# Hiding three of eight head groups of keys and queries in the padding rows of the other five

## The chip, the cores and the metric

The kernel runs on one core of one Trainium2 chip. The metric is device time in microseconds of one execution, the median of several runs. The profile shown is of one execution that was also timed.

## The reference

The model interleaves an attention block (A) and a token-mixing MLP (B), twice, over the same weights. There are S = 2048 tokens of D = 640, H = 32 heads of Dh = 20, and F = 1536. All arrays are bf16.

```python
def _A_ref(x, wqkv, wo):
    qkv = (x @ wqkv).reshape(B, S, 3, H, Dh)          # then split in q, k, v
    scores = jnp.einsum("bhqd,bhkd->bhqk", q, k) * (Dh ** -0.5)
    o = jnp.einsum("bhqk,bhkd->bhqd", softmax(scores), v)
    return o.transpose(0, 2, 1, 3).reshape(B, S, D) @ wo

def _B_ref(x, w1, b1, w2, b2):
    u = gelu(jnp.einsum("bsd,sf->bdf", layernorm(x), w1) + b1)
    return (jnp.einsum("bdf,fs->bds", u, w2) + b2).transpose(0, 2, 1)

x = x + _A_ref(layernorm(x), A_wqkv, A_wo)
x = x + _B_ref(layernorm(x), B_w1, B_b1, B_w2, B_b2)
# and both lines once more
```

Each layer has 32 heads times 2048 x 2048 scores, so 134 million exponentials.

## The kernel before, in words

**Heads in groups.** Four heads make a group, so there are NG = 8 groups. A head has 20 dimensions and takes a strip of 32 partitions: head j of a group lies on partitions 32j to 32j+19, and partitions 32j+20 to 32j+31 hold zeros. The padded weights are `wk_pad` and `wq_pad` (5 tiles of 128 input features, 8 groups, 128 columns); the padding columns are cleared by DVE (L1570) and ACT (L1579), and the others are copied in from `w_raw` (L1589 on ACT for groups 0 to 3, L1591 on DVE for groups 4 to 7). A projection (`proj_fill`, matmuls at L1199) multiplies one group's weights with 512 tokens of the normalised, transposed input `hT` (a view of `hh`), in five matmuls, and a copy (L377 for keys, L379 for queries, which also scales) brings the result from PSUM to `KT[:, g, tokens]` or `QTq[:, g, :]`. There are 8 groups times 4 blocks of tokens, for keys and for queries, in each layer.

**Scores and exponentials.** A cell is one head, 512 queries and 128 keys. `s_matmul` (L718) computes it as one matmul that contracts a strip of 32 partitions, at a position of the array of its own for each head of the group. Cells go into PSUM tiles `S` of three and two cells in turn, and ACT takes the exponential of a whole tile (L788, output `P`). Some cells go to DVE and POOL instead, by integer arithmetic on the bits of the number: they are computed into `Dt`, DVE takes them out (`ew`, L570), and a row of passes makes `ey` and then `Pd` (L600, L605, L623, L625), of which POOL can do parts (L676 for `ey`, L659 for `Pd`). [...] P times V (L1349) accumulates in `acc`, for four heads side by side.

**Order of the work.** The order on every engine is written by a planner in Python that runs while the program is built. It keeps its own clock for PE, DVE and ACT and puts "fills" (projections, output projection, first MLP matmuls) into the holes that PE has between scores, by due times. Where PE has been less busy than a floor (`FLOOR`, over `SPAN_US` = 3.413 us of its clock), it adds waves of four matmuls with zero weights (`zero_wave`, L777). A score matmul counts there as a quarter of the array. The DMAs on SP's queue are ordered by the framework; each waits on one of eight semaphores in turn, so for the DMA eight places ahead of it.

**Early runs.** Each attention starts before all tokens are there: groups 0 to 3 (`EG = 4`) and query blocks 0 and 1 are computed as tokens come in. Their partial sums lie in the parts of `KT` that belong to groups 4 to 7 (`part_view`), which are projected when the early runs of a block have ended. In layer 0 (`TokenFeed`) the tokens come from the input, in 16 tiles of 128 (`x0in`): each is normalised on DVE (L901 to L922) with a power on POOL (`rstd`, L918), transposed on PE, and projected. In layer 1 (`MixFeed`) they come from the MLP of layer 0. The weights `wk_pad` and `wq_pad` are built once, in layer 0.

**First MLP matmuls.** Rows of w1 times the normalised tokens (L1090, "mm1", accumulated by DVE at L1098) run as fills in three parts, by the tokens that are already there; `mid_rows` says how many of the 12 rows are begun before the last tokens are known.

## Time and profile before

| | |
|---|---|
| median of 3 runs | 1747.16 us (1746.76 to 1747.34) |
| the profiled execution's own time | 1747.74 us |
| span of its profile, first to last instruction | 1745.7 us |
| ACT exponentials (L788) | 1428 tiles, 1615.9 us busy |
| attention of layer 0, first to last exponential | 16.23 to 815.50 us |
| attention of layer 1, exponentials | 852.03 to 1675.9 us |
| projections of K and Q (L1199) | 243 + 237 matmuls into misc, 43 + 49 into Dt recorded |
| zero waves into acc (L777) | 4112 matmuls, 320.1 us busy |
| DVE copies of K and Q (L377, L379) | 64 + 64, about 0.68 us each |
| POOL passes for Pd (L659) | 337 of 0.62 us |

Times are microseconds from the first instruction of the span. "Busy" of a group is the time in which at least one of its instructions ran; the mean duration of one is longer where they overlap. A matmul's duration includes its way through the array, and the next one starts before it ends. PE's waits for weights ("PEld ... issue") are no loss by themselves.

### The profile page before, as it was taken

Reading aid. Unit: us, or ns where it says so; the run is one execution under the profiler, and the core shown is the slowest. Engines: PE = TensorE matmul, PEld = TensorE weight load, DVE = VectorE, ACT = ScalarE, POOL = GpSimd, SP = SyncE. Lnnn points to the kernel's source line nnn. Section 1 sums busy time; section 2 is a strip of 40 time slices with the busy share of each in tenths; the row PEclk is TensorE's granted clock in tenths of the full one; section 3 lists DMA queues with packets and bytes.
Section 4 is the critical chain, followed back from the end, with each engine's and each line's share of the span. In section 5 each row is a group of like instructions: output and inputs, shape, how many; then the busy total and the mean of one; then the engine's idle time right before and its main releaser. Section 6 shows DMA issues by size and latency. Waiting matters only on the chain.

```text
span 1745.7 us, 42946 instructions
## 1 busy us (share of the span) xinstructions
PE 1660.8 (95%) x17674; PEld 664.5 (38%) x17756; DVE 1541.2 (88%) x2511; ACT 1665.7 (95%) x1497; POOL 593.5 (34%) x952
## 2 busy tenths in 40 slices
PE   8999999999999999999999999999999999999999
PEld 3333333333333344444534433333333333444455
DVE  8789999999999999998544479999999999999973
ACT  9999999999999999999789999999999999999970
POOL 3133443443444333342000023434435443433310
PEclk9999999999999999999999999999999999999999
DMA  5000000000122010133412200001001220211245
GB/s 131 15 14 1 1 2 2 24 24 2 35 67 82 26 36 14 40 86 109 145 49 75 70 6 2 1 2 39 24 2 61 69 75 17 92 30 29 79 126 174
DMA packets 103060, 81.84 MB, mean 47 GB/s; under 512 B 51024, under 2 KB 87504, under 8 KB 102864
## 3 DMA queue, kind: packets, MB, share of 16 engines
q1 hardware_dynamic: 97328, 71.22, 13.8%
q0 software_dynamic: 5536, 7.88, 1.5%
q8 instruction: 138, 2.26, 0.6%
q14 instruction: 58, 0.48, 0.1%
HBM read 55.48 MB, written 23.59 MB: 45 GB/s over the span
## 4 chain that ended last, share of the span: by engine, by line
ACT 52%; PE 23%; issue 23%; DVE 1%; DMA 0%; SPq 0%; another core or an unknown queue 0%; POOL 0%; ACTq 0%; DVEq 0%
ACT P L788 52%; PE S L718 7%; PE acc L1349 3%; PE ya L1804 2%; PE misc L1199 2%; PE acc L777 2%; PE misc L1090 2%; PE Dt L1199 1%; PE um L1791 1%; PE ya L1813 1%; PE yb L1804 1%; PE misc L1177 1%; PE misc L1223 0%; PE Dt L1723 0%; DMA x0in<-in_A_x_dram 0%
## 5 line engine op out<-in xcount | busy, mean ns | idle before, releaser
L788 ACT ACTIVATE P<-S 128x1536 bf16<-128x1536 f32 (+1 forms) x1428 | 1615.9, 1370 | 10.6 <-PE S L718 10.3
L718 PE MATMUL S<-QTq,KT 32*128 32x512 bf16 (+1 forms) x4456 | 577.2, 336 | 66.9 <-ACT P L788 49.6
L676 POOL TENSOR_SCALAR ey<-ew 128x512 f16<-128x512 uint16 x511 | 317.3, 621 | 622.4 <-DVE ey L605 257.7
L718 PEld LDWEIGHTS <-KT 32*128 32x128 bf16 x5140 | 233.6, 91 | 523.4 <-issue 494.3
L570 DVE TENSOR_SCALAR ew<-Dt 128x512 int32<-128x512 f32 x528 | 359.4, 681 | 22.9 <-PE Dt L718 14.8
L1349 PE MATMUL acc<-P,Vaug 128*32 128x512 bf16 (+1 forms) x4436 | 362.1, 343 | 0.3 <-issue 0.3
L605 DVE SCALAR_TENSOR_TENSOR ey<-ey,ew 128x1024 int16<-128x1024 f16 x264 | 331.6, 1256 | 1.6
L777 PE MATMUL acc<-zr,zw 128*32 128x512 bf16 x4112 | 320.1, 383 | 1.2 <-POOL zr L155 1.2
L659 POOL TENSOR_SCALAR Pd<-ew 128x512 int16<-128x512 int16 x337 | 208.1, 620 | 233.6 <-DVE ey L605 74.9
L718 PE MATMUL Dt<-QTq,KT 32*128 32x512 bf16 (+1 forms) x684 | 202.9, 333 | 0.0
L600 DVE TENSOR_TENSOR ey<-ey 128x1024 f16<-128x1024 f16 x264 | 190.1, 720 | 1.5 <-POOL ey L676 0.3
L1349 PEld LDWEIGHTS <-Vaug 128*32 128x32 bf16 x5120 | 102.1, 94 | 171.8 <-issue 160.1
L777 PEld LDWEIGHTS <-zw 128*32 128x32 bf16 x4328 | 109.5, 96 | 92.8 <-issue 48.7
L623 DVE TENSOR_TENSOR Pd<-Pd,ey 128x1024 int16<-128x1024 int16 (+1 forms) x196 | 126.5, 645 | 6.4 <-POOL Pd L659 4.8
L625 DVE SCALAR_TENSOR_TENSOR Pd<-ew,ey 128x1024 int16<-128x1024 int16 (+1 forms) x123 | 122.4, 995 | 0.0
L918 POOL TENSOR_TENSOR rstd<-veps,mhalf 128x1 f32<-128x1 f32 x60 | 44.9, 749 | 210.9 <-DVE veps L916 188.6
L1349 PE MATMUL acc<-Pd,Vaug 128*32 128x512 bf16 (+1 forms) x684 | 103.7, 336 | 0.2 <-DVE Pd L623 0.2
L1199 PE MATMUL misc<-hh,wq_pad 128*128 128x512 bf16 x243 | 73.9, 383 | 2.8 <-issue 1.4
L1090 PEld LDWEIGHTS <-w1st 128*128 128x128 bf16 x672 | 52.4, 97 | 58.1 <-issue 45.4
L1199 PE MATMUL misc<-hh,wk_pad 128*128 128x512 bf16 x237 | 71.8, 383 | 2.2 <-issue 1.6
L1139 PE MATMUL misc<-wo_pad,attnT 128*128 128x320 bf16 x384 | 72.8, 302 | 0.0
L1090 PE MATMUL misc<-x1last,w1st 128*128 128x320 bf16 x384 | 71.4, 302 | 0.0
(144 smaller groups left out, 1187.4 us busy)
## 6 DMA issues: line engine op xcount, KB each, us to landing
w2s<-in_B_w_dram SPq DMA_DIRECT2D x16, 768.0 KB
uacc<-ustg POOLq DMA_DIRECT2D x24, 320.0 KB, 2.6
x1in<-xd SPq DMA_DIRECT2D x24, 320.0 KB
w1st<-in_B_w_dram SPq DMA_DIRECT2D x24, 256.0 KB
xd<-x2s SPq DMA_DIRECT2D x16, 320.0 KB
xin<-xd SPq DMA_DIRECT2D x16, 320.0 KB
w1st<-in_B_w_dram SPq DMA_DIRECT2D x21, 192.0 KB
xd<-x1s SPq DMA_DIRECT2D x12, 320.0 KB
```

What stands on the lines that cost most here:

```text
L570: nc.vector.tensor_scalar(out=w[:, slot, :], in0=Dt[:, :], scalar1=127.0 * FIX, scalar2=0.0, op0=ALU.add, op1=ALU.max)
L600: nc.vector.tensor_tensor(out=y, in0=y, in1=y, op=ALU.mult)
L605: nc.vector.scalar_tensor_tensor(out=box["t"][:, 0:512 * k], in0=y[:, 0:512 * k], scalar=MANT_C * MANT_K ** 2, in1=frac, op0=ALU.add, op1= ...
L623: nc.vector.tensor_tensor(out=bits, in0=bits, in1=t, op=ALU.add)
L659: after_vector(nc.gpsimd.tensor_scalar(out=bits, in0=whole, scalar1=128.0, scalar2=0.0, op0=ALU.mult, op1=ALU.add))
L676: return engine.tensor_scalar(out=out_ap, in0=in_ap, scalar1=MANT_K / FIX, scalar2=-MANT_K * MANT_S, op0=ALU.mult, op1=ALU.add)
L718: pe(nc.tensor.matmul(out_ap[:, c0:c0 + w], lhsT=KT[32 * j:32 * j + 32, g, kt * 128:(kt + 1) * 128], rhs=get_QT(st, qb)[32 * j:32 * j + 32 ...
L777: pe(nc.tensor.matmul(bank[32 * j:32 * j + 32, 0:w], lhsT=zw[:], rhs=zr[:, :, 0:64].to_broadcast([128, w // 64, 64]), start=start, stop=st ...
L788: nc.scalar.activation(out=P[:, 0:ncs, :].rearrange("p a b -> p (a b)"), in_=St[:, 0:ncs, :].rearrange("p a b -> p (a b)"), func=ACT.Exp, ...
L1090: pe(nc.tensor.matmul(t[:, 0:w], lhsT=w1_of[(p, ft)][:, sti, :], rhs=rows_in[sti][:, c0:c1], start=(sti == 0), stop=(sti == n_in - 1)))
L1199: pe(nc.tensor.matmul(t[:, :], lhsT=wpad[:, dt_, g, :], rhs=hT[:, dt_, tb * 512:(tb + 1) * 512], start=(dt_ == 0), stop=(dt_ == NDT - 1)))
L1349: pe(nc.tensor.matmul(acc[32 * j:32 * j + 32, a0:a0 + w], lhsT=Vaug[:, (kt * H + hh_) * VW:(kt * H + hh_) * VW + 32], rhs=P[:, slot, c0:c0 ...
```

## The change

Only groups 0 to 4 (`NP = 5`) are projected. The 12 padding rows of each of their strips now hold dimensions of the heads of groups 5, 6 and 7 (`HIDDEN`): 12 dimensions of group 5 in the gaps of group 0, 8 in those of group 1, and so on. The same five matmuls produce both. DMAs on SP's queue (`carry`, one for each strip) then move these rows to the places of groups 5 to 7 in `KT` and `QTq`, over partitions: 28 DMAs for the keys of a layer, 28 for each of the four query blocks.

Scores now contract the 20 rows of a head (`32 * j + DH`), because the rows behind them hold other heads' data.

In layer 0 the first projections of group 0 (the first 512 tokens) run before the gaps of its weights are filled; for these tokens two extra projections (`apart_fill`) are made later into tiles `apart`. The gaps are filled by 14 small copies on POOL, so the second half of the raw weights is now loaded before the input tiles 4 and 5. The padding is no longer cleared, but for group 0.

The partial sums of the early runs move (`homes`): block 0 into the parts of groups 4 and 6, block 1 into 5 and 7; the late groups are computed in the order 6, 4, 5, 7. A move is issued when its sources have been copied from PSUM and its place is free, and the planner books `MOVE_US`, 0.4 us for each DMA and 3.0 us to land. `mid_rows` of layer 0 goes from 0 to 2.

```diff
+NP = 5
+GAP = 32 - DH
+HIDDEN = {5: ((0, 0, 12, 0), (1, 0, 8, 12)), 6: ((2, 0, 12, 0), (3, 0, 8, 12)),
+          7: ((4, 0, 12, 0), (1, 8, 4, 12), (3, 8, 4, 16))}
+MOVE_US = (0.4, 3.0)
...
-    wq_pad = wperm.tile([128, NDT, NG, 128], BF16, name="wq_pad")
-    wk_pad = wperm.tile([128, NDT, NG, 128], BF16, name="wk_pad")
+    wq_pad = wperm.tile([128, NDT, NP, 128], BF16, name="wq_pad")
+    wk_pad = wperm.tile([128, NDT, NP, 128], BF16, name="wk_pad")
+    apart = [wperm.tile([128, 512], BF16, name=f"apart{i}") for i in range(2)]
...
+        homes = {EQ[0]: (4, 6), EQ[1]: (5, 7)}
+        rest = [6, 4, 5, 7]
...
-                pe(nc.tensor.matmul(out_ap[:, c0:c0 + w], lhsT=KT[32 * j:32 * j + 32, g, kt * 128:(kt + 1) * 128],
-                                    rhs=get_QT(st, qb)[32 * j:32 * j + 32, g, q0:q0 + w], start=True, stop=True,
+                pe(nc.tensor.matmul(out_ap[:, c0:c0 + w], lhsT=KT[32 * j:32 * j + DH, g, kt * 128:(kt + 1) * 128],
+                                    rhs=get_QT(st, qb)[32 * j:32 * j + DH, g, q0:q0 + w], start=True, stop=True,
...
+        def carry(dst, src, c0, c1, first, n, dim):
+            for j in range(4):
+                nc.sync.dma_start(out=dst[32 * j + dim:32 * j + dim + n, c0:c1],
+                                  in_=src[32 * j + DH + first:32 * j + DH + first + n, c0:c1])
...
+        def move_keys(L):
+            need = [("K", p[0], tb) for p in HIDDEN[L] for tb in range(NQB)]
+            if feed.regap and L == 5:
+                need.append(("G", 0))
+            owner = next(qb for qb in EQ if L in homes[qb])
+
+            def free():
+                return (feed.gate_late() and all(k in drained for k in need) and
+                        not any(qg[0] == owner for qg in early_left))
...
         def proj_fill(kind, g, tb, prio, ready, gate=None, fed=False):
+            if g >= NP:
+                return
...
     class TokenFeed:
         groups = 4
+        regap = True
...
-        mid_rows = 0
+        mid_rows = 2
...
             load_w(self.wv[:, 0], 2 * D)
+            load_raw(0, 1)
+            load_raw(1, 1)
             for tt in range(4, 6):
                 load_x(tt)
...
+            def gap_copies(i, tile_):
+                for L, parts in HIDDEN.items():
+                    for t_, first, n, dim in parts:
+                        if t_ == tile_:
+                            src = raw[(i, 1)][:].rearrange("p a (h i) -> p a h i", i=DH)[:, :, 4 * (L - 4):4 * (L - 4) + 4, dim:dim + n]
+                            nc.gpsimd.tensor_copy(out=gap_of(i, tile_, first, n), in_=src)
...
+            gaps_at(10.8, [(0, 1)])
+            gaps_at(12.0, [(1, 1), (0, 2), (1, 2), (0, 3), (1, 3)])
+            gaps_at(19.0, [(0, 4), (1, 4)])
+            gaps_at(19.0, [(0, 0), (1, 0)], lambda: ("K", 0, 0) in cx.kready and ("Q", 0, 0) in cx.kready)
```

More of the change, by code (lines that the diff above doesn't have):

```diff
@@ L384, in attention @@
         part_rows = (EG + 1) // 2
-        part_at = {qb: NG - part_rows * (i + 1) for i, qb in enumerate(EQ)}
-        rest = [g for qb in EQ for g in range(part_at[qb], part_at[qb] + part_rows)]
-        rest += [g for g in range(EG, NG) if g not in rest]
+        assert EG == 4 and len(EQ) == 2 and part_rows == 2
+        homes = {EQ[0]: (4, 6), EQ[1]: (5, 7)}
+        rest = [6, 4, 5, 7]
         order_left = ([(1, g) for g in range(EG) if NQB > 1 and 1 not in EQ] +
@@ L796, in part_view @@
         def part_view(qg):
-            v = KT[:, part_at[qg[0]]:part_at[qg[0]] + part_rows, :].rearrange("p a s -> p (a s)").bitcast(F32)
-            return v[:, 512 * qg[1]:512 * (qg[1] + 1)]
+            v = KT[:, homes[qg[0]][qg[1] // 2], :].bitcast(F32)
+            return v[:, 512 * (qg[1] % 2):512 * (qg[1] % 2 + 1)]
         def norm_rank(run):
@@ L1191, in enqueue_outproj_last, with apart_of @@
                     add_fill("O", 500.0, mms, evac, w, ready=ready, gate=lambda: low_left[0] == 0)
+        moves = []
+        def carry(dst, src, c0, c1, first, n, dim):
+            for j in range(4):
+                nc.sync.dma_start(out=dst[32 * j + dim:32 * j + dim + n, c0:c1],
+                                  in_=src[32 * j + DH + first:32 * j + DH + first + n, c0:c1])
+        def apart_of(i, tile_, tb):
+            return apart[i] if feed.regap and tile_ == 0 and tb == 0 else None
@@ new lines, in move_keys, with issue @@
+        def move_keys(L):
[6 more added lines that the diff above has]
+                        not any(qg[0] == owner for qg in early_left))
+            def issue():
+                for tile_, first, n, dim in HIDDEN[L]:
+                    cut = 512 if apart_of(0, tile_, 0) is not None else 0
+                    if cut:
+                        carry(KT[:, L, :], apart[0], 0, cut, first, n, dim)
+                    carry(KT[:, L, :], KT[:, tile_, :], cut, S, first, n, dim)
+                at = moved_at(L, need, 8 if feed.regap and L == 5 else 0)
+                for tb in range(NQB):
+                    kready[("K", L, tb)] = at
+            moves.append((free, issue))
@@ new lines, in move_queries, with free, issue @@
+        def move_queries(L, qb):
+            need = [("Q", qb, p[0]) for p in HIDDEN[L]]
+            if feed.regap and L == 5 and qb == 0:
+                need.append(("G", 1))
+            def free():
+                return feed.gate_late() and all(k in drained for k in need)
+            def issue():
+                q = get_QT(st, qb)
+                for tile_, first, n, dim in HIDDEN[L]:
+                    src = apart_of(1, tile_, qb)
+                    carry(q[:, L, :], q[:, tile_, :] if src is None else src, 0, 512, first, n, dim)
+                kready[("Q", qb, L)] = moved_at(L, need)
+            moves.append((free, issue))
@@ new lines, in attention, with moved_at, run_moves, apart_fill @@
+        queue = [0.0]
+        def moved_at(L, need, more=0):
+            queue[0] = max([pem["t"], queue[0]] + [drained[k] for k in need]) + MOVE_US[0] * (4 * len(HIDDEN[L]) + more)
+            return queue[0] + MOVE_US[1]
+        def run_moves():
+            for m in list(moves):
+                if m[0]():
+                    moves.remove(m)
+                    m[1]()
+        drained = {}
+        def apart_fill(i, prio):
+            wpad = (wk_pad, wq_pad)[i]
+            mms = []
+            for dt_ in range(NDT):
+                def mm(t, dt_=dt_):
+                    pe(nc.tensor.matmul(t[:, :], lhsT=wpad[:, dt_, 0, :], rhs=hT[:, dt_, 0:512],
+                                        start=(dt_ == 0), stop=(dt_ == NDT - 1)))
+                mms.append(mm)
+            def evac(t, end, eng):
+                copy_on(eng, apart[i][:], t[:, :], q_scale if i else None)
+            def after(end):
+                drained[("G", i)] = end + DVE_TO_PE
+            add_fill(("G", i), prio, mms, evac, 512, after=after, act=0.6, gate=lambda: feed.gate_late() and (i, "gap0") in cx.w_at)
@@ L1193, in proj_fill @@
         def proj_fill(kind, g, tb, prio, ready, gate=None, fed=False):
+            if g >= NP:
+                return
             wpad, key = (wk_pad, ("K", g, tb)) if kind == "K" else (wq_pad, ("Q", tb, g))
+            if feed.regap:
+                wi = int(kind == "Q")
+                mark = (wi, "gap0") if g == 0 and tb > 0 else (wi, g)
+                gate0 = gate
+                gate = lambda: mark in cx.w_at and (gate0 is None or gate0())
             scale = None if kind == "K" else q_scale
@@ L1207, in after @@
             def after(end):
-                kready[key] = end + DVE_TO_PE
+                kready[key] = drained[key] = end + DVE_TO_PE
             add_fill(key, prio, mms, evac, 512, ready=ready, after=after, act=0.6, gate=gate, fed=fed)
@@ L1213, in enqueue_qproj @@
                   for g in range(NG) if qb == LASTQB or (qb, g) in place}
-            for g in sorted(at, key=lambda g: at[g]):
-                proj_fill("Q", g, qb, at[g] - 10.0, 0.0)
+            first = {g: min(at[L] for L in [g] + list(HIDDEN) if L in at and (L == g or any(p[0] == g for p in HIDDEN[L])))
+                     for g in range(NP) if ("Q", qb, g) not in drained and g in at}
+            for g in sorted(first, key=lambda g: first[g]):
+                proj_fill("Q", g, qb, first[g] - 10.0, 0.0)
+            for L in HIDDEN:
+                if L in at:
+                    move_queries(L, qb)
         def v_fill(tt, part, wv_ap, prio, ready, fed=False, gate=None):
@@ L1259, in after @@
                 if all(4 * tb + i in tready for i in range(4)):
-                    for g in list(range(EG)) + rest:
+                    if tb == 0:
+                        for L in HIDDEN:
+                            move_keys(L)
+                            move_queries(L, 0)
+                        if feed.regap:
+                            for i in range(2):
+                                apart_fill(i, when(4, 0) - 4)
+                    for g in range(NP):
                         gate = feed.gate_late if g >= EG else None
-                        owner = next((qb for qb in EQ if part_at[qb] <= g < part_at[qb] + part_rows), None)
+                        owner = next((qb for qb in EQ if g in homes[qb]), None)
                         if owner is not None:
@@ L1406, in slot_work @@
             pump(pem["t"] + PE_TO_DVE)
+            run_moves()
             feed_ended()
@@ L1439, in attention @@
                            add_fill=add_fill, when=when, v_fill=v_fill, proj_fill=proj_fill, enqueue_qproj=enqueue_qproj,
-                           kready=kready, vready=vready, base=base, rest=rest, tready=tready, s_start=s_start, KT=KT,
+                           kready=kready, vready=vready, moves=moves, base=base, rest=rest, tready=tready, s_start=s_start, KT=KT,
                            Dbank=Dbank, misc=misc, spare=spare, warm_bank=warm_bank, acc_free=acc_free, pe_wave=pe_wave,
@@ L1515, in __init__ @@
                 "p (h a d) -> p h a d", h=2, a=NDT)
-            self.second = 2 * (NG - self.groups)
+            self.second = 4
         def wv_early(self, dt_):
@@ L1560, in load_rest, with gap_of @@
             def load_rest():
-                load_raw(0, 1)
-                load_raw(1, 1)
                 load_w(self.wv[:, 1], 2 * D + D // 2)
             landing = {tt: 3.2 + 0.5 * tt for tt in range(4)}
-            landing.update({4: 9.5, 5: 10.0})
+            landing.update({4: 12.0, 5: 12.5})
             wpads = (wk_pad, wq_pad)
-            def pads(i, part):
-                return wpads[i][:].rearrange("p a g (j i) -> p a (g j) i", i=32)[:, :, 16 * part:16 * part + 16, DH:32]
-            cx.submit(cx.Proc(0, [(0.46, lambda e, i=i: nc.vector.memset(pads(i, 0), 0.0), 0.0) for i in range(2)], 0.9))
+            def gap_of(i, tile_, first, n):
+                return wpads[i][:, :, tile_, :].rearrange("p a (j i) -> p a j i", i=32)[:, :, :, DH + first:DH + first + n]
@@ new lines, in begin @@
+            cx.submit(cx.Proc(0, [(0.2, lambda e, i=i: nc.vector.memset(gap_of(i, 0, 0, GAP), 0.0), 0.0) for i in range(2)], 0.9))
+            def gap_copies(i, tile_):
[4 more added lines that the diff above has]
+                            nc.gpsimd.tensor_copy(out=gap_of(i, tile_, first, n), in_=src)
@@ new lines, in gaps_at, with issue @@
+            def gaps_at(time, pairs, extra=None):
+                def issue():
+                    for n, (i, tile_) in enumerate(pairs):
+                        gap_copies(i, tile_)
+                        if tile_ == 0:
+                            cx.w_at[(i, "gap0")] = cx.pem["t"]
+                        elif tile_ == 4:
+                            self.second -= 1
+                        else:
+                            copied_gap[(i, tile_)] = cx.pem["t"] + 0.8 * (n + 1)
+                            if (i, tile_) in copied_main:
+                                cx.w_at[(i, tile_)] = max(copied_main[(i, tile_)], copied_gap[(i, tile_)])
+                cx.moves.append((lambda: cx.pem["t"] >= time and (extra is None or extra()), issue))
@@ L1572, in zero_values @@
+            copied_main, copied_gap = {}, {}
+            gaps_at(10.8, [(0, 1)])
+            gaps_at(12.0, [(1, 1), (0, 2), (1, 2), (0, 3), (1, 3)])
+            gaps_at(19.0, [(0, 4), (1, 4)])
+            gaps_at(19.0, [(0, 0), (1, 0)], lambda: ("K", 0, 0) in cx.kready and ("Q", 0, 0) in cx.kready)
             def zero_values(e):
@@ L1578, in begin @@
                                                                      func=ACT.Identity, bias=1.0, scale=1.0), -0.06)] +
-                              [(0.5, lambda e, i=i: nc.scalar.memzero(pads(i, 1)), -0.06) for i in range(2)],
-                              2.1, eng=cx.acm))
+                              [], 2.1, eng=cx.acm))
             def group_copy(i, g):
@@ L1593, in done @@
                 def done(e):
-                    cx.w_at[(i, g)] = e + 0.05
+                    copied_main[(i, g)] = e + 0.05
+                    if g in (0, 4):
+                        cx.w_at[(i, g)] = e + 0.05
+                    elif (i, g) in copied_gap:
+                        cx.w_at[(i, g)] = max(copied_main[(i, g)], copied_gap[(i, g)])
                     self.second -= g >= self.groups
@@ L1597, in group_copy @@
                 cx.submit(cx.Proc((1.2 if g == 0 else 1.5) if g < self.groups else 5, [(0.5, copied, 0.0)], ready, eng=eng, after=done))
-            for g in range(NG):
+            for g in range(NP):
                 for i in range(2):
@@ L1628 @@
         groups = 4
+        regap = False
         paired = 16
```

## The prediction

> **What bounds the kernel now.** I read the page from the top: the busy shares, then the span in 40 slices.

> ```profile
> PE 1660.8 (95%) x17674; PEld 664.5 (38%) x17756; DVE 1541.2 (88%) x2511; ACT 1665.7 (95%) x1497; POOL 593.5 (34%) x952
> ...
> PE   8999999999999999999999999999999999999999
> ...
> ACT  9999999999999999999789999999999999999970
> ...
> PEclk9999999999999999999999999999999999999999
> ```

> PE and ACT are equally busy, so the shares don't say which one sets the time. The windows of the two attention stretches do (columns: span, PE, PEld, DVE, ACT and POOL busy with counts, granted clock, DMA share, GB/s):

> ```profile
> 0.00:10.00 10.00, 8.82 (x108) 4.12 (x108) 6.66 (x23) 8.60 (x13) 4.39 (x15) 1.00 0.82 248
> 5.00:9.00 4.00, 4.00 (x63) 2.00 (x59) 3.30 (x13) 3.33 (x6) 2.15 (x4) 1.00 1.07 337
> 16.23:815.50 799.27, 761.68 (x8394) 292.71 (x8432) 759.55 (x1203) 799.12 (x707) 310.26 (x492) 1.00 0.12 32
> 855.00:1676.00 821.00, 784.03 (x8317) 308.65 (x8350) 710.36 (x1147) 814.20 (x719) 272.24 (x433) 1.00 0.13 40
> ```

> From 16.23 to 815.50 ACT is busy 799.12 of 799.27 us; in the second layer it is idle only near the start. PE leaves 38 and 37 us free in them. ACT's waits say the same: 10.3 us for PE in the whole run, of which 3.9 is one wait.

> ```profile
> ACT P L788 <- PE S L718: 10.3, 11, 3.9
> ```

> So what counts is how many exponentials ACT has left, when its first one starts, and whether anything makes it wait. PE time taken away is worth nothing by itself. The costliest groups give the prices:

> ```profile
> L788 ACT ACTIVATE P<-S 128x1536 bf16<-128x1536 f32 (+1 forms) x1428 | 1615.9, 1370 | 10.6 <-PE S L718 10.3
> ...
> L659 POOL TENSOR_SCALAR Pd<-ew 128x512 int16<-128x512 int16 x337 | 208.1, 620 | 233.6 <-DVE ey L605 74.9
> ...
> L777 PE MATMUL acc<-zr,zw 128*32 128x512 bf16 x4112 | 320.1, 383 | 1.2 <-POOL zr L155 1.2
> ...
> L1199 PE MATMUL misc<-hh,wq_pad 128*128 128x512 bf16 x243 | 73.9, 383 | 2.8 <-issue 1.4
> ...
> L1199 PE MATMUL misc<-hh,wk_pad 128*128 128x512 bf16 x237 | 71.8, 383 | 2.2 <-issue 1.6
> ```

> Last, the timeline where the first exponential is released and where SP issues many small DMAs:

> ```profile
> 10.85 0.49 DVE L901 BATCH_NORM_STATS2 bnst<-x0in 128x6 f32<-128x320 bf16 x1 [1.54 <-DMA x0in<-in_A_x_dram]
> ...
> 14.29 0.68 DVE L377 CAST KT<-Dt 128x512 bf16<-128x512 f32 x1
> 14.89 0.68 DVE L379 TENSOR_SCALAR QTq<-misc 128x512 bf16<-128x512 f32 x1
> ...
> 16.23 2.37 ACT L788 ACTIVATE P<-S 128x1536 bf16<-128x1536 f32 x2 [2.87 <-PE S L718]
> ...
> 37.01 8.26 SPq L208 DMA_DIRECT2D wo_pad<-in_A_wo_dram  x21
> ```

> **PE: projections out, zero waves in.** The order of the built program has 230 fewer K and Q projection matmuls (115 K, 115 Q; the ten for the two extra tiles are taken off). Five span 1.24 us at 13.25, of which the last alone is 0.38, so one costs PE (1.24-0.38)/4 = 0.215 us, all of them 49. But the planner keeps PE's recent work at a floor, and it fills the holes: zero matmuls rise by 912 (836 in acc, 76 elsewhere), 228 waves of four. 56 of them took 3.21 us at 818.59, so a wave is 0.23 us and the refill 52 us. PE's load is what it was.

> **DVE: fewer copies, but POOL loses its hosts.** 46 copies of 0.68 us (L377, L379) go: -31.4 us, and six padding copies of 0.27: -1.6. The planner starts a POOL pass only beside a DVE step of at least 0.45 us that takes no port lock, such as one of these copies. With 46 hosts gone, POOL's Pd passes (L659) fall from 337 to 296, and DVE does that work itself: 32 full adds of 0.728 less, 23 half adds of 0.432, 11 full multiply-adds of 1.25 and 23 halves of 0.681 more: +16 us. Four more exponential tiles on DVE cost about 7, four more mm1 additions 2. DVE is relieved by some 8 us in 1541; it bounds nothing here.

> **ACT.** All of that relief has to arrive as fewer ACT tiles, and the order shows how few: one 1536-wide and one 1024-wide tile less, one 512-wide more, 3568 to 3564 cells. At 1615.9/3568 = 0.453 us a cell this is **-1.8 us**, on the path. Two clears of the padding (0.93 and 0.60 us at 5.4) go too, but ACT then waits 0.67 us for a transpose: nothing.

> **Start.** Two weight loads, 819 KB, move on SP's queue ahead of the input tiles 4 and 5. In before DVE had tile 4 at 10.85. At 337 GB/s (the window 5 to 9) they add 2.4 us, at the 193 GB/s that the window 10 to 20 shows 4.2. DVE's new order puts three statistics (0.4 each) of tiles 4 and 5 ahead of the first K copy, and 0.5 us of others ahead of the first Q copy: 13.3 + 1.2 + 0.6 + 0.5 + 0.7 = 16.3, where the Q copy ended at 15.57. So the first exponential comes **+0.7 us** later, and since ACT has no hole behind it until 815, all of it counts. Slow end: +2.4. Fast end: the tile isn't late; the V copy now stands earlier, so the Q matmuls start at about 12.4 instead of 13.25 and the whole chain gains up to 1.2. I take 0.7, by the window nearest to the loads.
> POOL gets 14 small gap copies. Ten stand ahead of the rstd of tiles 4 to 6; no row shows them; by L659 (512 elements, 0.62 us) they take 2.9 us by size to 6.2 by count. DVE then waits up to 2.8 us for rstd, with the K and Q copies of group 1 behind it. Those are needed by the seventh exponential tile, some 7 us after the first, so I take 0; without that cover +1.0.

> **Moves.** 284 DMAs of 4 to 12 partitions, all on SP. Issue is 8.26/21 = 0.39 us each, 112 us of a queue that is mostly idle. What matters is the distance from a move to the first scores that read it, counted in exponential tiles (1615.9/1428 = 1.13 us each) in the order: keys of groups 6, 5, 7 have 34, 39 and 59 tiles in layer 0, and 16, 37 and 58 in layer 1; query moves have 90 or more. The tightest, keys 6 of layer 1, has 18.1 us for eight DMAs: 3.1 us of issue and one landing (2.6 us in the row of the uacc stores, 4.1 and 5.0 for the two bias loads). Hidden: 0. Behind the moves on SP stand x0in, x1in, w2s, w1st and the x stores; the order puts those of the layer 1 start (w2s at 866.86 in before) behind queries copied by 860.6, and the x2s store of tile 8 (920.58) behind 24 moves of queries copied by 896.8, issued by 906. Also 0.

> **Scores over 20 rows.** No row has 20. A weight load of 32 rows takes 91 ns, of 128 rows 97; a 512-column matmul 379 and 383 ns. Rows don't set its time: 0.

> **Ends of layers.** Two mm1 rows are begun earlier in layer 0, so no mm1 addition is left behind the last transposes (0.45 us at 817.53). It lay beside a wait for PE: 0, at most -0.45.

> **Sum:** -1.8 + 0.7 = -1.1. The profiled execution took 1747.74 (span 1745.7), 0.58 over the median of 1747.16; so 1746.6 for it and **1746.1** as the median. Ends: -1.8-1.2-0.45 = -3.45, 1743.7; -1.8+2.4+1.0 = +1.6, 1748.8.

> **Rivals.** About 0.2%, 3.5 us, is what a measurement of this kernel can tell from no change.
> *Moves that land one after another (slower, 0.10).* SP's DMAs share eight semaphores in turn, each waiting for the eighth before it. If these small copies serialise, keys 6 of layer 1 need eight landings: at 2.6 us 20.8 and ACT waits 2.7, at 4.1 us 32.8 and it waits 14.7; totals 1749 to 1761. It decides from 18.1/8 = 2.3 us per DMA. Against it: they are issued 0.39 us apart and the DMA share is 0.12.
> [...]
> *The clock (slower, 0.10).* If the throttle counts the rows in use, scores now count 20 for 32. Scores (3084 matmuls of 512 columns, 2056 of 256, at 0.215 and 0.108 us on a quarter of the array) are 221 of 1746 us of it, 12.7%; 4.8 points are lost, while the planner still books each as a quarter and holds its floor of 0.52. A stretch as long as the planner's window (SPAN_US, 3.4 us) at half rate would cost 1.7 us of PE; three decide, 14 (3% of the two attentions) give 24 us: 1770. Against it: 1.00 in every window, and zero waves in the projections' place.
> [...]
> *A start that gains (faster, 0.20).* Tile 4 isn't late and every fast end holds: about 1743.5, and beyond the 3.5 if the freed DVE gives back some tenths more.

> **How the numbers follow.** Forecast 0.55, all within 0.2%; faster rival 0.20 (0.18 beyond the line); the two slower ones 0.20; something unseen on the slow side 0.05. So faster 0.18, same 0.57, slower 0.25. The range runs from below the fast end, 1742.8, into the lower half of the late moves, 1752.5; the clock and the worst moves stay out.

> **What would show it.** 1426 exponential tiles, ACT busy about 1614 and no new wait in either attention; first exponential at 16.9 (start term); tile 4's statistics at about 13.3; POOL's L659 near 296; zero matmuls up, PE as busy; PEclk all 9. Wrong if ACT waits for PE near the first scores of group 6 in layer 1, if PEclk drops, or if the first exponential is past 18.6 or before 15.

## Result, and the profile after

The changed kernel takes 1749.12 us (median; 1747.55 to 1755.86) against 1747.13 for the kernel before, run beside it: a ratio of 1.0014, 95% interval 1.0008 to 1.0020. It is slower by some 2 us. Its profiled execution took 1750.07, span 1748.3.

The page after, its busy shares and the groups that the prediction priced:

```profile
PE 1677.4 (96%) x18430; PEld 662.5 (38%) x18430; DVE 1537.9 (88%) x2501; ACT 1663.7 (95%) x1494; POOL 569.3 (33%) x926
...
PEclk9999999999999999999999999999999999999999
...
L794 ACT ACTIVATE P<-S 128x1536 bf16<-128x1536 f32 (+2 forms) x1427 | 1614.9, 1359 | 14.2 <-PE S L724 13.3
...
L783 PE MATMUL acc<-zr,zw 128*32 128x512 bf16 x4948 | 381.9, 384 | 1.2 <-POOL zr L160 1.2
...
L665 POOL TENSOR_SCALAR Pd<-ew 128x512 int16<-128x512 int16 x296 | 182.4, 617 | 238.4 <-DVE ey L611 65.8
```

One exponential tile less, ACT's exponentials 1.0 us shorter, POOL's `Pd` passes at 296, zero matmuls up: the work moved as the built order had said. But ACT waits 13.3 us for scores (before: 10.3), and PE is busy 17 us longer. Not all of the 17 is real: the profile of before lacks the records of 82 matmuls (17674 of the 17756 that the same order shows in another run), 68 of them projections. A run further down (32 rows, moves held back) has the changed kernel's PE order, as many records and a full clock, and PE is busy 1671.0 us in it: 6.4 less than here. The row of clocks shows only nines, because a slice of it is 44 us long. Windows of the stretches in question show more (span, PE, PEld, DVE, ACT and POOL busy with counts, granted clock, DMA share, GB/s):

```profile
6.80:37.60 30.80, 28.12 (x233) 10.91 (x225) 25.00 (x72) 27.66 (x32) 15.35 (x30) 1.00 0.54 120
37.60:47.80 10.20, 10.20 (x53) 2.33 (x45) 4.50 (x13) 6.89 (x7) 1.11 (x2) 0.50 0.48 90
47.80:78.50 30.70, 29.50 (x238) 10.43 (x240) 19.52 (x33) 30.66 (x28) 4.32 (x7) 1.00 0.05 13
78.50:81.90 3.40, 3.40 (x18) 0.64 (x10) 2.69 (x6) 2.61 (x3) 1.81 (x3) 0.50 0.34 98
```

For 13.6 us the clock was at half (a score matmul of 512 columns took 0.60 us there on average, 0.38 at full clock). PE had no free time in these stretches, and ACT, which has no other gap over 0.25 us in this attention, was busy 6.89 of 10.20 and 2.61 of 3.40 us.

Stage by stage, after against before: first exponential 15.81 against 16.23 (-0.4); layer 0 from first to last exponential 803.84 against 799.29 (+4.55, of which ACT's idle gaps at 39, 43, 47 and 82 us make 4.28); between the attentions -0.1; layer 1 822.90 against 823.91 (-1.0); the tail -0.4. Sum +2.6, the difference of the spans. By and large the runs go with the clock: the changed kernel's at a mean clock of 0.999 took 1747.6 to 1748.7, those at 0.996 took 1750 to 1750.7, the two at 0.993 and 0.994 took 1755.9. The kernel before was at 1.000 in its profile. For its runs beside the experiments below the clock is on record: 1.000 in 104 of 111, 0.999 in the others.

### The profile page after: what moved, and what is told of

Read it like the earlier page. It is cut to its first block, busy times and chain, and to the rows that moved or that the text cites. A ratio compares the mean times of both kernels' runs of the same rounds, so it can differ in the third digit from the quotient of the medians.

```text
span 1748.3 us, 44712 instructions
## 1 busy us (share of the span) xinstructions
PE 1677.4 (96%) x18430; PEld 662.5 (38%) x18430; DVE 1537.9 (88%) x2501; ACT 1663.7 (95%) x1494; POOL 569.3 (33%) x926
## 4 chain that ended last, share of the span: by engine, by line
ACT 54%; issue 25%; PE 19%; DVE 2%; DMA 0%; POOL 0%; SPq 0%; ACTq 0%; DVEq 0%
ACT P L794 54%; PE S L724 5%; PE ya L1938 2%; PE acc L1451 2%; PE misc L1096 2%; PE acc L783 1%; PE misc L1289 1%; PE um L1925 1%; PE ya L1947 1%; PE yb L1938 1%; PE Dt L1289 0%; DMA x0in<-in_A_x_dram 0%; PE misc L1145 0%; PE misc L1318 0%; PE misc L1857 0%
## 5 line engine op out<-in xcount | busy, mean ns | idle before, releaser
L794 ACT ACTIVATE P<-S 128x1536 bf16<-128x1536 f32 (+2 forms) x1427 | 1614.9, 1359 | 14.2 <-PE S L724 13.3
L724 PE MATMUL S<-QTq,KT 20*128 20x512 bf16 (+1 forms) x4446 | 578.2, 337 | 59.1 <-ACT P L794 41.6
L724 PEld LDWEIGHTS <-KT 20*128 20x128 bf16 x5132 | 228.9, 91 | 522.8 <-issue 493.3
L783 PE MATMUL acc<-zr,zw 128*32 128x512 bf16 x4948 | 381.9, 384 | 1.2 <-POOL zr L160 1.2
L665 POOL TENSOR_SCALAR Pd<-ew 128x512 int16<-128x512 int16 x296 | 182.4, 617 | 238.4 <-DVE ey L611 65.8
L724 PE MATMUL Dt<-QTq,KT 20*128 20x512 bf16 (+1 forms) x686 | 204.6, 334 | 0.0
L783 PEld LDWEIGHTS <-zw 128*32 128x32 bf16 x5240 | 131.3, 96 | 116.3 <-issue 65.0
L631 DVE SCALAR_TENSOR_TENSOR Pd<-ew,ey 128x1024 int16<-128x1024 int16 (+1 forms) x157 | 151.2, 963 | 0.0
L1145 PE MATMUL misc<-wo_pad,attnT 128*128 128x320 bf16 x384 | 71.8, 302 | 0.0
L831 DVE STREAM_TRANSPOSE T<-acc 128x512 f32<-128x512 f32 (+1 forms) x78 | 54.2, 695 | 13.5 <-PE acc L1451 13.3
L1096 PE MATMUL misc<-hh,w1st 128*128 128x320 bf16 x282 | 51.8, 302 | 0.0
```

Source lines behind the costliest of these rows:

```text
L631: nc.vector.scalar_tensor_tensor(out=bits, in0=whole[:, lo:hi], scalar=128.0, in1=t, op0=ALU.mult, op1=ALU.add)
L665: after_vector(nc.gpsimd.tensor_scalar(out=bits, in0=whole, scalar1=128.0, scalar2=0.0, op0=ALU.mult, op1=ALU.add))
L724: pe(nc.tensor.matmul(out_ap[:, c0:c0 + w], lhsT=KT[32 * j:32 * j + DH, g, kt * 128:(kt + 1) * 128], rhs=get_QT(st, qb)[32 * j:32 * j + DH ...
L783: pe(nc.tensor.matmul(bank[32 * j:32 * j + 32, 0:w], lhsT=zw[:], rhs=zr[:, :, 0:64].to_broadcast([128, w // 64, 64]), start=start, stop=st ...
L794: nc.scalar.activation(out=P[:, 0:ncs, :].rearrange("p a b -> p (a b)"), in_=St[:, 0:ncs, :].rearrange("p a b -> p (a b)"), func=ACT.Exp, ...
L1096: pe(nc.tensor.matmul(t[:, 0:w], lhsT=w1_of[(p, ft)][:, sti, :], rhs=rows_in[sti][:, c0:c1], start=(sti == 0), stop=(sti == n_in - 1)))
```

## Experiments

Three theories: **rows** (the granted clock follows the rows in use, so 20 for 32 can bring it down), **start** (the two weight loads ahead of input tiles 4 and 5), **moves** (the new DMAs on SP). The expectations name a fourth, order: that the new order of the fills thins PE's early stretches and rows don't count.

**Rows alone.** In the kernel before, `s_matmul` contracts 20, 26 or 8 rows in place of 32; nothing else changes. With 8 rows, 12 of a head's 20 dimensions are left out.

```diff
-lhsT=KT[32 * j:32 * j + 32, g, ...]
-rhs=get_QT(st, qb)[32 * j:32 * j + 32, g, ...]
+lhsT=KT[32 * j:32 * j + DH, g, ...]                  # or + 26, or + 8
+rhs=get_QT(st, qb)[32 * j:32 * j + DH, g, ...]
```

> The kernel before, with one edit: scores contract 20 rows of each strip in place of 32 (the 12 left out are zeros, so the result is the same). No projection, move or order changes. Theory rows (the granted clock follows the rows in use, so scores over 20 rows count for less and some early stretches fall below what keeps the clock up): the clock falls below 1.000 between about 30 and 100 us, in one to four stretches of 3.4 us, ACT waits for PE there by 0.5 to 1.6 us a gap, and the time is 1748.5 to 1752. Theory order (what thins the early stretches is the new order of fills, and rows are not counted): clock 1.000, no new wait, 1747.1 within 0.7.

> The kernel before with scores over 26 rows in place of 32 (rows 20 to 31 hold zeros, so the scores are the same). With 20 rows it took 1754.7 at clocks of 0.992 to 0.997. If the gate weighs PE's work by the rows in use, half the step takes less than half of that, since fewer windows fall under the line: 1747.5 to 1750.5 with clocks of 0.997 to 1.000. If any number below 32 counts alike (a tile size rounded up or down), it takes 1747.1 as before or 1754.7 as with 20 rows.

> The kernel before with scores over only 8 of the 20 rows of a head (12 dimensions are left out of the scores). Same order. Theory rows: scores count for a quarter of what they did, the clock falls in many more stretches than with 20 rows, mean clock 0.90 to 0.98 and 1765 to 1850 us. Theory order: clock 1.000, 1747.

| rows | us | granted clock | ratio to before |
|---|---|---|---|
| 32 (before, medians beside the others) | 1746.96, 1747.10 | 0.999 to 1.000 | |
| 26 | 1747.36 (1746.42 to 1750.54) | 0.997 to 1.000 | 1.0004 (0.9995 to 1.0012) |
| 20 | 1754.70 (1750.05 to 1756.58) | 0.992 to 0.997 | 1.0049 (1.0035 to 1.0062) |
| 8 | 1779.03 and 1825.82 | 0.975, 0.942 | none |

With 20 rows the kernel is slower than the 1748.5 to 1752 expected, and in its profile the clock fell in layer 1, at 882.8 and 1002.3 us, for 3.4 and 6.8 us. The mean clock of that run, 0.997, leaves no room for a third stretch at 30 to 100.

The matmul itself costs the same. The groups of PE with forms kept apart, before and then with 20 rows (busy, mean ns):

```profile
L718 PE MATMUL S<-QTq,KT 32*128 32x512 bf16 x2712 | 433.0, 379 | 54.9 <-ACT P L788 42.0
```

```profile
L718 PE MATMUL S<-QTq,KT 20*128 20x512 bf16 x2712 | 434.0, 380 | 50.1 <-ACT P L788 37.2
```

What differs is the clock that follows. The same windows of layer 1, before, then with 20 rows:

```profile
998.90:1002.30 3.40, 2.51 (x32) 1.09 (x31) 3.10 (x10) 3.40 (x4) 0.55 (x1) 1.00 0.82 250
1002.30:1009.10 6.80, 6.35 (x52) 2.62 (x45) 3.22 (x7) 6.80 (x8) 0.00 (x0) 1.00 0.44 97
```

```profile
998.90:1002.30 3.40, 2.51 (x32) 1.23 (x33) 3.10 (x9) 3.40 (x4) 0.55 (x1) 1.00 0.76 232
1002.30:1009.10 6.80, 6.80 (x32) 1.80 (x27) 1.66 (x4) 5.16 (x5) 0.00 (x0) 0.50 0.46 106
```

In the first window of each, PE is busy 2.51 of 3.40 us with 32 matmuls; with 20 rows the next 6.8 us run at half clock. PE's busy share does not tell the two kernels apart, the rows do.

What the clock answers to can be estimated from the records. In the profile of the changed kernel, the last 8 us left out, it changes only at whole multiples of 3.413 us from its first change (6.84, then 37.56, 47.80, 78.52 and 81.93); the kernel before has its first at 5.78 and no other. So both can be cut into windows of that length from there on. Count every matmul in a window by the rows and columns that it occupies, at 0.2155 us for 512 columns of input (the spacing of the zero waves at full clock), as a share of the whole array. The windows ahead of the changed kernel's two drops had 0.38 and 0.37 of the array in use. Of the 1006 other windows at full clock, after which the clock stayed, one had as little (0.38, in the kernel before), and the next 0.41. By rows alone 49 of them had no more than the fuller of the two, by the time that PE was busy 29. So columns seem to count with the rows, and the clock fell after windows near 0.38. This is the author's estimate, from the two drops in these two profiles alone; some 0.5% of the matmuls have no record in the profile of before, and what brings the clock back is not in it.

With 8 rows the drop shows in the page's row of clocks itself:

```profile
PEclk9775799999999999999999999999999958997999
```

26 rows cost almost nothing (0.4 us), 20 rows 7.6 us, 8 rows 32 or more: not a price per row. By the estimate above, windows would come down to the level of the two drops one after another: of the 507 in before's own profile, 1 has 0.39 or less of the array in use; with its scores counted at 26, 20 and 8 rows it is 2, 6 and 13. Rows is shown, on this kernel; its order is that of before, so the order theory doesn't explain it.

**The changed kernel with 32 rows, and with the tiles loaded first.** One kernel contracts 32 rows in groups 0 to 4 (it adds the hidden heads' products, so its scores are others). One loads tiles 4 and 5 ahead of the second weight halves, with the order on every compute engine unchanged. One does both.

```diff
+            rows = 32 if g < NP else DH
-lhsT=KT[32 * j:32 * j + DH, g, ...]
+lhsT=KT[32 * j:32 * j + rows, g, ...]
```

```diff
+            for tt in range(4, 6):
+                load_x(tt)
             load_raw(0, 1)
             load_raw(1, 1)
-            for tt in range(4, 6):
-                load_x(tt)
```

> The changed kernel, with scores of groups 0 to 4 contracting 32 rows again (the 12 further rows hold other heads' data, so these scores have added products in them; groups 5 to 7 keep 20). The order of all instructions stays. Theory rows: the clock is 1.000 throughout, the four gaps at 39 to 83 us (4.3 us in the profile) are gone, and the time is about 1750.1 - 4.3 = 1745.8, below before. Theory order: clock 0.993 to 0.999 as in the changed kernel, 1749 median.

> The changed kernel with one thing put back: input tiles 4 and 5 are loaded ahead of the second halves of the key and query weights again. Every compute engine's order of instructions is the changed kernel's. If the load order is what costs the changed kernel its time (start theory), the statistics of tile 4 start at 10 to 11 us in place of 12.4 to 14.2, the first exponential at 15.0 to 15.5, and the time falls from 1749.1 to about 1747, with a granted clock of 1.000 in most runs. If the clock gate counts the rows in use (rows theory), the start gains the same 0.5 to 1.5 us, but stretches at half clock inside the attention stay: 1748 to 1748.7, and clocks of 0.995 to 0.999 in most runs.

> The changed kernel with the load order of before and with scores over 32 rows in groups 0 to 4 (it then adds products of the hidden heads to the scores of those groups, so its scores are others; the work is the same). With both suspected costs out, rows and start theory together expect the change's own worth: 1746.0 to 1746.8, below before by 0.3 to 1.1, granted clock 1.000 but for a rare stretch in groups 5 to 7, which still have 20 rows. If something else costs the time (the moves, the gap copies), it stays near 1748.

| | 20 rows | 32 rows in groups 0 to 4 |
|---|---|---|
| weight halves first | 1749.12, 1.0014 (1.0008 to 1.0020) | 1747.93, 1.0005 (0.9996 to 1.0014) |
| tiles 4 and 5 first | 1747.90, 1.0007 (0.9999 to 1.0016) | 1745.76, 0.9993 (0.9984 to 1.0001) |

Each of the two is worth 1 to 2 us by the medians, though single steps overlap in their intervals; the two corners, 1.0014 and 0.9993, don't. 32 rows alone missed the expected 1745.8 at a clock of 1.000: its clocks are 0.997 to 1.000, and in its profile PE was slow already before the first exponential at 18.20 us: five V matmuls took 1.49 us at 16.12, where five had taken 0.85 at 10.02. With both repaired, the runs lie close (1745.23 to 1747.46) and nine of eleven have a clock of 1.000. The load order alone leaves a wide spread, 1745.39 to 1752.32: full clock in three of eleven runs, and those three took 1745.4 to 1745.7.

First exponentials: 15.81, 18.20, 16.70 and 15.65 us in the four profiles with the weight halves first (the third and fourth are of kernels described below), 14.4 to 15.2 in the six of whole hiding with the tiles first. In the second and third PE was slow around it: the five V matmuls above, and in the third five key matmuls in 2.31 us at 16.87, where five had taken 1.24 at 11.17. So part of what a late start costs goes through the clock as well. The wait that the prediction had set at 0 with its cover also came up. With the tiles first and 20 rows, the second query half landed late, and POOL's gap copies held up the power behind them:

```profile
14.36 0.52 POOL L1681 COPY wq_pad<-w_raw 128x160 bf16<-128x160 bf16 x2 [2.11 <-DMA w_raw<-in_A_wqkv_dram]
...
16.41 1.07 POOL L924 TENSOR_TENSOR rstd<-veps,mhalf 128x1 f32<-128x1 f32 x2
...
16.99 0.96 DVE L928 TENSOR_SCALAR h_bf<-x0in,mv,rstd 128x640 bf16<-128x640 bf16 x2 [2.18 <-POOL rstd L924]
...
17.88 0.68 DVE L383 CAST KT<-misc 128x512 bf16<-128x512 f32 x1
...
18.61 0.57 PE L1318 MATMUL misc<-x1last,hh 128*128 128x320 bf16 x3 [0.72 <-DVE KT L383]
```

The bracket is the idle time and its end: the copy waits 2.11 us for the weights, DVE 2.18 us for `rstd`, and the key copy and PE's V matmuls queue behind it. PE's window at that time, then the same window with 32 rows, where the weights came earlier:

```profile
17.70:21.10 3.40, 1.71 (x12) 0.53 (x10) 3.40 (x11) 2.92 (x3) 0.09 (x1) 1.00 0.72 196
```

```profile
17.70:21.10 3.40, 3.36 (x26) 1.30 (x26) 3.40 (x13) 3.40 (x4) 1.71 (x5) 1.00 0.56 159
```

PE was busy for half of it, and the clock then fell at 21.1 us, for 10.2 us. ACT itself had idled 0.4 us in the stall; it lost 4.5 in the gaps that followed.

**More zero waves.** The planner books a score matmul as a quarter of the array, as 32 rows would be. Booked as 20 of 128 rows (the line below and two more like it), it finds PE below its floor more often and adds 452 zero matmuls.

```diff
-pe_wave("S", dep, cells=0.25 * len(tiles[t]))
+pe_wave("S", dep, cells=DH / 128 * len(tiles[t]))
```

> The changed kernel, whose planner books a score matmul as 20/128 of the array in place of a quarter; the order has 460 zero matmuls (115 waves) more and the same ACT tiles. Theory rows: clock 1.000, the gaps are gone, and the time is 1744.5 to 1746.5 unless the added waves make ACT wait. Theory order: more zero waves would also help, so this run does not tell the two apart; it tells what the loss is worth and whether a repair is to be had by waves. Theory late moves: 1749, no change.

> A version with both repairs, doing the whole computation: the changed kernel with input tiles 4 and 5 loaded first again, and with its planner booking a score matmul at 20 of 128 rows, so that it adds zero waves (452 zero matmuls) where the floor asks for them. Rows and start theory: the start is that of the load-order run (first exponential 14.5 to 15.0), no stretch at half clock at 16 to 20 us as booking alone had, a clock of 1.000 in most runs. Its undisturbed runs: booking alone's 1748.2 to 1749.1 less some 2 us of start = 1746.2 to 1747.0; median 1746.6, a little below before. If zero waves cost more than the gate does, it stays at 1748 or above with a clock of 1.000.

> As the version with both repairs, but the 20-row booking holds only for the first 110 us of layer 0, where the load-order run fell to half clock (21 to 31 and 42 to 48 us): 44 more zero matmuls in place of 452. Rows theory: if these 11 waves lift the weak stretches over the line, the clock is 0.999 to 1.000 and the time 1745.5 to 1746.3, below before by 0.7 to 1.5. If they don't, it takes what the load-order run took, 1747.9, with its spread of 1745.4 to 1752.3.

Booking alone: 1750.13, ratio 1.0021 (1.0012 to 1.0030). With the tiles first: 1750.21, 1.0017 (1.0008 to 1.0026). Only in the first 110 us, with the tiles first: 1746.49, 1.0000 (0.9991 to 1.0009). Over the whole run the repair failed: 1744.5 to 1746.5 and 1746.6 were expected. In the second kernel the runs at full clock took 1747.1 to 1747.4, so the waves themselves cost some 1.7 us over the 1745.4 to 1745.7 of the load-order kernel, and eight of eleven runs still had a clock under 1.000. The short one is level with before and just outside the 1745.5 to 1746.3 expected; its gain of 1.3 us over the load-order kernel, each against before, is within the intervals. Why the weak stretches stay weak in spite of the waves was not settled.

**Moves.** In one kernel every move is issued twice. In two others (the short booking with tiles first, and 32 rows with tiles first) layer 0's query moves wait until all 16 input tiles have been taken in, and all of its moves stay behind the DVE work issued by then; the order on the compute engines is again unchanged.

```diff
+                for again in range(2):
                     nc.sync.dma_start(out=dst[...], in_=src[...])
```

```diff
-return feed.gate_late() and all(k in drained for k in need)
+return feed.gate_late() and all(k in drained for k in need) and (not feed.regap or len(tready) == NT)
...
+                if feed.regap:
+                    after_vector(inst)
```

> The changed kernel with every one of the 284 moves issued twice, the second copy writing the same values again. If the moves are hidden, the time stays at the changed kernel's 1749.1 (1748 to 1750.5, by the clock of each run). If they are late for the scores (moves theory), the tightest cover, the keys of group 6 in layer 1 with 18.1 us, now has 16 DMAs: ACT waits for PE ahead of the first scores of that group, and the time rises by 3 us or more.

> The version with input tiles 4 and 5 first and the early 20-row booking, and layer 0's query moves held back on SP until all 16 input tiles have been taken in; every compute engine's order is unchanged. In the runs so far four moves (2.7 us on SP) stood ahead of the loads of input tiles 10 and 11, DVE then waited 2.2 to 2.3 us for a tile (0.2 in before), and ACT lost 0.7 and 0.4 us right behind it, also at full clock. If that is the moves' cost, it goes: no DVE wait over 0.5 us for an input tile at 36 to 40 us, about 1 us less, and one weak stretch of PE less for the clock: 1745.3 (1744.5 to 1746.0), below before by 1.5. If the tiles are late for their buffers' sake, it takes 1746.5 as without it.

> The same hold on layer 0's query moves in the kernel with 32-row scores in groups 0 to 4 and tiles 4 and 5 first (its scores hold added products, as there). With the clock out of it: 1744.7 (1744.2 to 1745.3) if the moves cost 1.1 us, 1745.8 as without the hold if they cost nothing.

Twice the moves took 1792.68 (1786.52 to 1797.65), ratio 1.0267 (1.0252 to 1.0283). But not by waits for the first scores of group 6: SP's queue and DVE's timeline show what was late.

```profile
440.09 40.12 SPq L1204 DMA_DIRECT2D QTq<-QTq  x55
480.26 0.44 SPq L1159 DMA_DIRECT2D xd<-x1s  x1
480.75 0.43 SPq L1129 DMA_DIRECT2D xin<-in_A_x_dram  x1
...
483.29 0.49 DVE L1157 TENSOR_TENSOR x1s<-misc,xin 128x320 f32<-128x320 f32 x1 [13.30 <-DMA xin<-in_A_x_dram]
```

55 moves hold the queue for 40.12 us, 0.73 us each, and the load of `xin`, which DVE needs for the output of block 0, stands behind them. ACT then lost 13.2 us in one gap, and PE came out of it slow: a score matmul took 0.61 us at 484.46, where it had taken 0.39 at 469.74. Two more places are of this kind: ACT lost 6.6 us in one gap at 47 us, where DVE had waited 7.68 us for an `x0in` tile, and 6.1 at 1367 us, where it had waited 6.27 for `xin`.

The single moves of the changed kernel do this too, on a small scale. Its SP queue and DVE at the third block of tokens, and after them SP's queue before:

```profile
34.44 2.69 SPq L1203 DMA_DIRECT2D QTq<-QTq  x4
37.23 0.86 SPq L1655 DMA_DIRECT2D x0in<-in_A_x_dram  x2
...
39.51 0.49 DVE L907 BATCH_NORM_STATS2 bnst<-x0in 128x6 f32<-128x320 bf16 x1 [2.24 <-DMA x0in<-in_A_x_dram]
```

```profile
35.25 0.36 SPq L1551 DMA_DIRECT2D x0in<-in_A_x_dram  x1
35.65 0.36 SPq L208 DMA_DIRECT2D wo_pad<-in_A_wo_dram  x1
36.61 0.35 SPq L1551 DMA_DIRECT2D x0in<-in_A_x_dram  x1
```

Four moves of 0.67 us put both input tiles off to 37.23, and DVE waits 2.24 us (0.19 before). At full clock ACT loses 1.1 us behind such a tile, as the kernel with 32 rows and tiles first shows (DVE waits 2.26 us there):

```profile
40.64 2.37 ACT L795 ACTIVATE P<-S 128x1536 bf16<-128x1536 f32 x2 [0.74 <-PE S L725]
...
43.39 1.45 ACT L795 ACTIVATE P<-S 128x1536 bf16<-128x1536 f32 x1 [0.39 <-PE S L725]
```

Holding the moves back takes this away. With 32 rows and the moves held:

```profile
34.02 0.36 SPq L1658 DMA_DIRECT2D x0in<-in_A_x_dram  x1
34.42 0.35 SPq L214 DMA_DIRECT2D wo_pad<-in_A_wo_dram  x1
35.09 0.35 SPq L1658 DMA_DIRECT2D x0in<-in_A_x_dram  x1
...
36.33 0.49 DVE L908 BATCH_NORM_STATS2 bnst<-x0in 128x6 f32<-128x320 bf16 x1
```

The tile is there when DVE is; no bracket. ACT's two gaps are gone too. This kernel took 1745.04, ratio 0.9987 (0.9978 to 0.9995), faster than before; against the same kernel without the hold (0.9993) the intervals overlap. Its layer 0 is 0.9 us shorter than without the hold (799.01 against 799.94), both at full clock. With 20 rows, the short booking and the hold: 1744.7 to 1745.1 in the four runs at full clock, 1747.3 to 1748.8 in the seven others; median 1747.38, 1.0000 (0.9991 to 1.0009). The expected 1745.3 came only in the runs at full clock.

**Keys only.** Queries of all eight groups are projected, with zeros in their padding; only keys hide and move. A hidden key row then meets a zero, so groups 0 to 4 can contract 32 rows and nothing is added. Tiles first and held moves are kept. Its pair contracts 20 rows everywhere, with the same order of instructions and the same values.

```diff
-            if g >= NP:
+            if kind == "K" and g >= NP:
                 return
...
+            rows = 32 if g < NP else DH                 # the pair: rows = DH
```

> A version that does the whole computation: only the keys hide in padding rows, the queries of all eight groups are projected with zeros in theirs. A hidden key row meets a zero, so groups 0 to 4 can contract 32 rows again (groups 5 to 7 contract 20). Tiles 4 and 5 are loaded first and layer 0's moves wait for the tokens. It has half of the change's relief of ACT: 3566 cells against 3568 before and 3564, so -0.9 us. Rows theory: clock of 1.000 in nearly all runs and 1745.9 (1745.2 to 1746.5), below before by 0.6 to 1.7. If what slowed the changed kernel is the hiding itself and not the rows, it is at 1747 or above with clocks under 1.000.

> The keys-only version with 20 rows in all scores and nothing else changed: same order of instructions on every engine, same values. Rows theory: clocks of 0.996 to 0.999 in most runs, 1747.5 to 1750, its fastest runs (clock 1.000) as fast as the keys-only version's. If rows don't count: the keys-only version's time.

With 32 rows 1745.88 (1745.28 to 1748.30), ratio 0.9996 (0.9987 to 1.0005), clock 0.999 to 1.000 in nine of eleven runs. With 20 rows 1748.93 (1745.09 to 1753.76), 1.0008 (0.9997 to 1.0018), clock 0.994 to 0.998 in seven of eleven. At full clock they take 1745.3 to 1746.4 and 1745.1 to 1745.4; their layer stretches in the two profiles, both at full clock, are 799.606 and 823.496 against 799.604 and 823.492 us. So at full clock the rows cost nothing here. The medians are 3.05 us apart on the side that the rows theory expected, but the two intervals overlap: this pair alone doesn't show the loss, the pair of before with 20 rows does. Keys only is faster than the changed kernel (the intervals are apart), and its median is 1.2 us below before, which its interval doesn't separate from no change.

## Why the prediction was wrong

It said 1746.1. The measured 1749.12 lies inside its range, and 2 us is inside the 0.2% that it called no change, but the kernel is slower where a small gain was forecast. By its own steps:

**"Scores over 20 rows ... Rows don't set its time: 0"** is the step that failed. The observation was right: 379 and 380 ns. What it stood for was wrong, because with fewer rows the clock fell in the microseconds after: the term measures +1.2 to +2.1 us by the medians, not 0. The clock rival named this and got 0.10. Against it stood a clock of 1.00 in every window, which showed no more than that the kernel before, with 32 rows, had kept it; and the zero waves put in for the projections, which the planner sized by booking a score as a quarter of the array. The rival's size was off the other way: it took three stretches to decide and priced 14 at 24 us. The profile after has 13.6 us at half clock, four stretches of 3.4 us. The windows ahead of its two drops had 0.38 and 0.37 of the array in use, by the estimate above; with scores counted at 32 rows both would have had 0.42. ACT's gaps there are 4.28 us. Some 1.1 of them are the moves' (the two gaps at full clock above), so the clock's part is about 3.1: 0.23 us per us at half clock and not the 0.5 assumed. PE had 2.68 of 30.80 and 1.20 of 30.70 us free in the windows at full clock beside them, which may be why; no run tests it.

The stretches at half clock that the windows above show are 3.4, 6.8 and 10.2 to 10.3 us, one to three times 3.413. The windows with an equal 2.51 us of PE and unequal clocks after them say that PE's busy time alone doesn't decide it. The first change of the clock comes at 5.78 us of the span in the profile of before and at 6.84 in the changed kernel's, whose later ones lie on a grid of 3.413 us from there. If that grid lies differently in each execution of one kernel, the kernel could be slowed in some runs and not in others, as the 20-row kernels are (the changed kernel from 0.993 to 0.999); this is the author's estimate, and no run shows it.

**"Moves ... Hidden: 0"** was mis-sized by about 0.9 us. The issue was priced by rows of weight loads at 0.39 us; a move takes 0.64 (median) and 0.72 back to back (28 in 20.20 us), so SP is held some 183 us and not 112. No run here shows the moves landing one by one. The tightest cover was not the keys of group 6 in layer 1, before which ACT has no gap, but loads that stand behind moves and belong to other work: `x0in` of tiles 10 and 11, which the text named as standing behind the moves but priced for layer 1 alone, and `xin`, which it didn't name. In the changed kernel 28 moves end at 450.7, `xin` is issued at 451.32, and DVE uses it at 456.86, without a wait. The 0.9 us are layer 0 with and without the hold, at full clock (799.94 and 799.01).

**Start, "+0.7".** First exponential at 16.9 was forecast. The profiled run has 15.81 and tile 4 at 12.39 (forecast 13.3); the other three profiles with this load order have 12.23, 13.28 and 14.20 for the tile, and the four first exponentials have a mean of 16.6. But the 16.23 of before that the term was set against was itself late: the same start gave 15.05, 15.17 and 15.32 in the 20-, 26- and 8-row kernels. Between the means of four, 16.59 and 15.44, the load order and the new order of DVE cost 1.15. So the sign was right and the size near, with 2.6 us between the earliest and the latest of the four. The ten gap copies ahead of `rstd` take 2.85 us together, the low end of their pricing.

**ACT "-1.8"** holds within what can be measured. With rows (in groups 0 to 4), load order and moves out of the way, the whole hiding took 1745.04 against 1747.11, -2.1 (-3.8 to -0.9 by the interval). In the profiles the two attentions are 1.3 shorter (799.01 + 822.90 against 799.29 + 823.91). The rest fits the start: the six first exponentials with tiles first have a mean of 14.8 against the 15.4 above, which the prediction had as the fast end of its start term.

**PE, DVE, POOL** came nearly as read from the built order: 1427 tiles (the text said 1426, a slip against its own one-and-one less, one more), `Pd` at 296, 912 zero matmuls more, and DVE 3 us lighter where 8 were forecast. The lock of a DVE step is a rule of the planner (`locks` in the kernel); no run here tests it. PE is at 1671.0 where the clock stayed full; 1660.8 of before lacks the matmuls without a record. The page's 1660.8 and 1677.4 therefore don't show that PE's load rose. None of these bounds anything.

The sum by measured terms, each kernel's median taken against before beside it: own worth -2.1; moves about +0.9; then load order and rows, which come to +1.1 (0.94 for 1.99) and +2.1 (-1.20 for 0.94) when the load order is put right first, and to +1.2 for rows (0.83 for 1.99) and +2.0 for the load order (-1.20 for 0.83) the other way round. Either way the steps lead to the measured +2.0 because they are differences of the same four medians, so the sum is no check of its own. Neither rows nor the load order alone brings the median as high (1747.90 and 1747.93 against 1749.12). The load order was in the forecast with +0.7; rows and moves were there with 0.

## What to carry to other kernels

Before an edit that makes a matmul smaller without making it shorter (fewer rows, or padding cut away), look at how much of the array is in use, window by window: here the padding held the clock (1747.10 against 1754.70 us), and a clock of 1.00 before said nothing of the margin. By the estimate above the lowest window of before had 0.38 in use, as the windows ahead of the changed kernel's drops had. Price a new DMA by what stands behind it on its queue, not only by who waits for its data, and take its issue time from its own kind. Where a kernel's time follows the granted clock run by run, compare its runs at full clock first: they give the edit's own worth, the rest goes with the clock.
